# Phase one of a two-branch transformer layer: first-norm products put off behind the second norms of later tiles, five tiles transposed on TensorE instead of eight, six single tiles instead of four

## The chip, the cores and the metric

The kernel runs on one core of one Trainium2 chip. The metric is device time in microseconds (us). Every run of this case was in the fast state and on one core; the granted TensorE clock of a run lay between 0.997 and 1.000. A ratio is the mean time of one kernel's fast runs over the mean time of the other's fast runs of the same rounds, so it is not quite the ratio of the medians quoted beside it. In the profiles TensorE is PE, VectorE DVE and ScalarE ACT; POOL and SP are two more engines, and here they issue the DMAs of phase one, each from a queue of its own.

## The reference, cut to what matters

```python
def _layernorm(x, axis=-1, eps=1e-05):
    m = jnp.mean(x, axis=axis, keepdims=True)
    v = jnp.var(x, axis=axis, keepdims=True)
    return (x - m) / jnp.sqrt(v + eps)

def _B_ref(x, w1, w2, w3, w4):              # x: (1, 2048, 1024), bf16
    h = _gelu(_layernorm(x, axis=-1) @ w1)  # w1: (1024, 1024)
    ...                                     # shifts of rows, @ w2, second MLP with w3, w4
x = A_x
xn = _layernorm(x, axis=-1)                 # the first norm
return x + _A_ref(xn, ...) + _B_ref(xn, ...)
```

Branch B normalizes the already normalized `xn` again. The kernel computes both norms from one set of statistics of `x`: the "first norm" gives `xn` (needed in phase two and in branch A), the "second norm" gives the input of the product with `w1`.

## The kernel before: the parts that matter

The 2048 rows are 16 tiles of 128. Phase one computes `gelu(norm2(x) @ w1)`. For that each tile's second norm must be transposed: tiles 0 to 7 by matmuls with an identity on TensorE, tiles 8 to 15 by a DMA transpose that SP issues. The first norm of a tile, made on VectorE, does three things at once: it keeps `xn` on the chip, POOL writes it to a scratch in DRAM, and it frees the tile's x buffer, so that SP may load the x tile ten places on.

```python
def load_x(n):
    if n < NT:
        xts[n] = ring.tile([P, D], BF16, tag="xt", bufs=10, name=f"xt{n}")
        nc.sync.dma_start(xts[n][:], x_v[:, n, :])
# ... loads of x 0..9, w1, w2 are issued here ...

def norm_stats(n, part=None):                       # cut
    nc.vector.bn_stats(st[:, 0, :], xt[:, 0:512])
    nc.vector.bn_stats(st[:, 1, :], xt[:, 512:1024])
    nc.vector.bn_aggr(mv[:], st[:])
    nc.vector.scalar_tensor_tensor(ab[:], ...)
    nc.gpsimd.tensor_tensor(rr[:], ab[:], neghalf[:], op=ALU.pow)
    if n >= NPE:
        nc.gpsimd.tensor_scalar(nm2[:], ...)

def norm2(n, xn2T, jj):                             # second norm
    if n < NPE:                                     # on VectorE (NPE = 8)
        nc.vector.tensor_scalar(xn2[:, c], xts[n][:, c], ...)
    else:                                           # on ScalarE, then a DMA transpose
        nc.scalar.activation(xn2[:], xts[n][:], ACTF.Identity, bias=nm2[:], scale=rr[:, 1:2])
        nc.sync.dma_start_transpose(xn2T[:, jj], xn2[:])

def norm1(n):                                       # first norm
    nc.vector.tensor_scalar(xn, xts[n][:], ...)
    nc.gpsimd.dma_start(xn_v[:, n, :], xn)          # 256 KB to DRAM
    load_x(n + 10)                                  # 256 KB from DRAM, on SP's queue
    if n in (12, 15):
        load_w3()

for n in range(1, NPE):                             # tiles 1..7
    norm_stats(n + 1, 0); norm2_of(n); norm_stats(n + 1, 1)
    if n > 1:
        norm1(n - 2)                                # two tiles behind
    if n < 4:
        stage1(n - 1, 1, ...)                       # single tiles 0, 1, 2 (then 3)
for n0 in range(4, NT, 2):                          # pairs (4,5) .. (14,15)
    stage1(n0, 2, tiles2[n0], between)              # 8 groups of 8 matmuls, one GELU each
```

A "group" below is eight matmuls into one PSUM tile, ended by one GELU on ScalarE; a tile or a pair has eight groups.

## Time and profile before

| | before |
|---|---|
| time, median of 6 runs (lowest, highest) | 1521.69 us (1520.39, 1524.99) |
| span of the profiled run | 1519.6 us |
| TensorE busy | 1508.8 us, 99% |
| phase one's products on TensorE | 8.38 to 69.39 us |

From the page of the kernel before: busy times by engine (us, share of the span, instructions), the granted TensorE clock in 40 slices (9 is 90% or more), and the chain of work that ended last, by engine.

```profile
PE 1508.8 (99%) x9781; PEld 808.3 (53%) x9853; DVE 546.2 (36%) x1137; ACT 506.7 (33%) x1147; POOL 179.4 (12%) x248
...
PEclk9999999999999999999999999999999999999999
...
PE 98%; DMA 1%; issue 0%; DVE 0%; ACT 0%; SPq 0%; POOL 0%
```

TensorE is the bound: 99% busy, at full clock, and 98% of the chain. Only a wait of TensorE, or work taken from it, can move the time by much.

From the timeline of TensorE before (start in us, length, engine, line, operation, count). L292 is the transposing matmul, L303 the product with w1, L377 the first product of phase two.

```profile
16.03 0.39 PE L292 MATMUL ps<-c_ident_sb,xn 128*128 128x128 bf16 x4
16.25 0.61 PE L303 MATMUL ps<-xn2T,w_sb 128*128 128x128 bf16 x8
16.70 0.39 PE L292 MATMUL ps<-c_ident_sb,xn 128*128 128x128 bf16 x4
...
32.71 36.84 PE L303 MATMUL ps<-xn2T,w_sb 128*128 128x256 bf16 x336
69.39 5.78 PE L377 MATMUL ps<-w_sb,hTB 128*128 128x512 bf16 x25
```

Here is one tile's transposes, two halves of four matmuls, and then the pairs: 36.8 us of matmuls without a gap that the profile counts, and phase two at 69.39. Four transposing matmuls take 0.22 us (16.03 to 16.25), eight 128-column products 0.45 us (16.25 to 16.70).

Four stretches of the kernel before: start:end, length, then busy us and instruction count of PE, PEld, DVE, ACT and POOL, the granted clock, the mean busy share of the 16 DMA engines (it can come out a little over 1), and GB/s.

```profile
core 0: us, PE busy (x) PEld busy (x) DVE busy (x) ACT busy (x) POOL busy (x), PEclk, DMA share, GB/s
17.00:23.00 6.00, 5.99 (x106) 5.75 (x103) 5.85 (x14) 4.41 (x16) 3.78 (x5) 1.00 1.05 389
23.00:28.00 5.00, 4.92 (x74) 4.49 (x71) 4.84 (x12) 3.81 (x12) 2.71 (x5) 1.00 0.85 303
28.00:46.00 18.00, 18.00 (x175) 16.24 (x173) 17.43 (x43) 13.84 (x29) 14.40 (x24) 1.00 0.88 195
46.00:54.00 8.00, 8.00 (x75) 7.16 (x74) 1.44 (x4) 6.03 (x12) 3.23 (x6) 1.00 1.05 272
```

The last two columns are the ones to keep. DMA runs at 389 and 303 GB/s up to 28 us, when w2 and the x tiles come in, and less after that, when the transposes start.

### The profile page before, as it was taken

To read this page: it belongs to the slowest core of one execution; us is meant where nothing else is said; L and a number is where in the kernel's file an instruction comes from. 1 tells how busy PE (TensorE), PEld (TensorE's weight loads), DVE (VectorE), ACT (ScalarE), POOL (GpSimd) and SP (SyncE) were. 2 spreads that over 40 slices of the span, in tenths; PEclk is the share of its full clock that TensorE was granted. 3 is DMA by queue.
4 is the path that set the end of the run, shared out by engine and by line. 5 is a ranking of instruction groups with operands and counts; after the bars stand their busy time and mean duration, and the time that the engine had idled before them with its cause. 6 is when DMAs were issued, how large, how long until landed. Compare 5 with 4: busy or idle time off the path is not lost.

```text
span 1519.6 us, 24277 instructions
## 1 busy us (share of the span) xinstructions
PE 1508.8 (99%) x9781; PEld 808.3 (53%) x9853; DVE 546.2 (36%) x1137; ACT 506.7 (33%) x1147; POOL 179.4 (12%) x248
## 2 busy tenths in 40 slices
PE   9999999999999999999999999999999999999998
PEld 7844444445444444444466645654665555445555
DVE  7382230100120122222246614651664266416542
ACT  6533203013022011111256614650663266326630
POOL 5231020211111231100000010001000100010001
PEclk9999999999999999999999999999999999999999
DMA  8799762353355887532499947992997389628611
GB/s 283 157 266 317 220 174 93 136 201 111 126 169 141 198 281 255 192 133 70 137 240 253 238 117 189 244 238 79 228 240 190 118 223 217 185 76 209 175 46 53
DMA packets 306459, 274.20 MB, mean 180 GB/s; under 512 B 153787, under 2 KB 274128, under 8 KB 306088
## 3 DMA queue, kind: packets, MB, share of 16 engines
q1 hardware_dynamic: 284168, 189.92, 49.3%
q0 software_dynamic: 22032, 82.63, 15.9%
q8 instruction: 79, 1.29, 0.4%
q14 instruction: 36, 0.29, 0.1%
q10 hardware_dynamic: 144, 0.07, 0.0%
HBM read 190.98 MB, written 46.19 MB: 156 GB/s over the span
## 4 chain that ended last, share of the span: by engine, by line
PE 98%; DMA 1%; issue 0%; DVE 0%; ACT 0%; SPq 0%; POOL 0%
PE ps L651 30%; PE pso L709 14%; PE ps L577 14%; PE ps L519 13%; PE ps L545 13%; PE ps L377 4%; PE ps L303 3%; PE psS L666 2%; PE psO L690 2%; PE ps L836 1%; PE ps L469 1%; PE ps L434 0%; PE gps L448 0%; DMA wt<-in_A_Wq_dram 0%; DMA PT<-Pn 0%; PE warm L320 0%
## 5 line engine op out<-in xcount | busy, mean ns | idle before, releaser
L651 PE MATMUL ps<-hTb,wt 128*128 128x396 bf16 (+3 forms) x2528 | 500.4, 343 | 0.3 <-DMA wt<-in_A_Wq_dram 0.3
L651 PEld LDWEIGHTS <-wt 128*128 128x128 bf16 x2528 | 232.2, 98 | 167.6 <-DMA wt<-in_A_Wq_dram 0.7
L577 PE MATMUL ps<-wt,xT 128*128 128x512 bf16 x1003 | 220.1, 379 | 1.1
L709 PE MATMUL pso<-wo_sb,oX 128*128 128x512 bf16 x938 | 209.3, 379 | 1.2 <-issue 0.2
L519 PE MATMUL ps<-xn3T,w_sb 128*128 128x512 bf16 x896 | 196.2, 379 | 0.0
L545 PE MATMUL ps<-w_sb,h3T 128*128 128x512 bf16 x873 | 194.3, 379 | 1.2
L577 PEld LDWEIGHTS <-xT 128*128 128x128 bf16 x1024 | 100.2, 98 | 120.8
L520 ACT ACTIVATE h3T<-ps 128x512 bf16<-128x512 f32 x112 | 66.9, 597 | 290.4 <-PE ps L519 289.5
L709 PEld LDWEIGHTS <-oX 128*128 128x128 bf16 x960 | 92.6, 98 | 108.2
L657 ACT CAST KT<-ps 128x396 bf16<-128x396 f32 (+3 forms) x160 | 82.3, 514 | 186.9 <-PE ps L651 184.2
L545 PEld LDWEIGHTS <-h3T 128*128 128x128 bf16 x896 | 87.0, 98 | 103.4
L519 PEld LDWEIGHTS <-w_sb 128*128 128x128 bf16 x896 | 86.6, 98 | 102.1
L672 DVE TENSOR_REDUCE sums<-sm 99x4 f32<-99x396 f32 (+2 forms) x176 | 97.6, 555 | 113.0 <-ACT sm L670 113.0
L659 ACT ACTIVATE QT<-ps 128x396 bf16<-128x396 f32 (+3 forms) x160 | 84.2, 527 | 119.1 <-PE ps L651 102.0
L668 DVE TENSOR_TENSOR sm<-psS,c_mask_reg_sb 99x396 f32<-99x396 f32 x160 | 91.3, 571 | 86.3 <-PE psS L666 85.7
L579 ACT CAST Vs<-ps 128x512 bf16<-128x512 f32 x64 | 37.5, 587 | 233.1 <-PE ps L577 174.9
L670 ACT ACTIVATE sm<-sm 99x396 f32<-99x396 f32 (+2 forms) x176 | 92.9, 528 | 63.7 <-DVE sm L668 60.7
L583 DVE CAST Vs<-ps 128x512 bf16<-128x512 f32 x64 | 44.3, 692 | 170.0 <-PE ps L577 158.0
L678 DVE TENSOR_TENSOR Pn<-sm,rs 99x396 bf16<-99x396 f32 (+2 forms) x176 | 99.0, 562 | 7.2 <-DMA PT<-Pn 1.1
L546 DVE TENSOR_TENSOR R<-ps,R 128x512 f32<-128x512 f32 x32 | 21.9, 690 | 180.9 <-PE ps L545 166.6
L716 POOL DMA_DIRECT2D out_dram<-ot x30 | 16.4, 547 | 584.0 <-DVE ot L715 578.2
L715 DVE TENSOR_TENSOR ot<-pso,Rt 128x512 bf16<-128x512 f32 (+1 forms) x33 | 22.3, 676 | 172.3 <-PE pso L709 166.9
(120 smaller groups left out, 1072.0 us busy)
## 6 DMA issues: line engine op xcount, KB each, us to landing
wt<-in_A_Wq_dram SPq DMA_DIRECT2D x76, 512.0 KB
wt<-in_A_Wk_dram SPq DMA_DIRECT2D x76, 512.0 KB
wt<-in_A_Wv_dram POOLq DMA_DIRECT2D x24, 1024.0 KB, 6.5
V_scratch<-Vs SPq DMA_DIRECT2D x32, 512.0 KB
V<-V_scratch SPq DMA_DIRECT2D x32, 384.0 KB
R_scratch<-x POOLq DMA_DIRECT2D x16, 512.0 KB, 3.9
R<-R_scratch SPq DMA_DIRECT2D x16, 512.0 KB
R_scratch<-R POOLq DMA_DIRECT2D x16, 512.0 KB, 3.2
```

Source lines behind the costliest of these rows:

```text
L519: nc.tensor.matmul(ps[:].rearrange("p (n t) -> p n t", t=P), w3_sb[:, k, f * P:(f + 1) * P], xn3T[tb][:, :, k, :], start=(k == 0), stop=(k ...
L520: nc.scalar.activation(h3T[:, f, :], ps[:], ACTF.Gelu_apprx_tanh)
L545: nc.tensor.matmul(ps[:], h3T[:, f, j * P:(j + 1) * P], w4_sb[:, f, ch * 512:(ch + 1) * 512], start=(f == 0), stop=(f == FT - 1))
L577: nc.tensor.matmul(ps[:], xT[:, m4 * 4 + j, k, :], wv[:, k, :], start=(k == 0), stop=(k == KT - 1))
L651: nc.tensor.matmul(ps[:, :nb] if flat else ps[:, :nb].rearrange("p (t c) -> p t c", t=nt), w[:, k, hh * P:(hh + 1) * P], B["rhs"](k), star ...
L657: nc.scalar.copy(o, i)
L659: nc.scalar.mul(o, i, scale)
L668: nc.vector.tensor_tensor(sm[:T, :, :T], S3, t["mask"][:].unsqueeze(1).to_broadcast((T, 4, T)), op=ALU.add)
L670: nc.scalar.activation(e[:T, :, :T], sm[:T, :, :T], ACTF.Exp, scale=LN2)
L672: nc.vector.tensor_reduce(ss, e[:T, :, :T], axis=AX.X, op=ALU.add)
L678: nc.vector.tensor_tensor(Pn[:T, :, :T], e[:T, :, :T], rs[:T, :].unsqueeze(2).to_broadcast((T, 4, T)), op=ALU.mult)
L709: nc.tensor.matmul(self.ps[:, :self.w], self.oX[self.gl // 3][:, h, self.gl % 3 * P:(self.gl % 3 + 1) * P], wo_sb[:, h, self.cc], start=(h ...
```

## The change

The intent, as the code reads: TensorE's last waits in phase one are for second norms and their transposes, so VectorE should make second norms earlier and first norms later (they are needed only after 69 us). With second norms earlier, tiles 5, 6 and 7 can go through the DMA transposes, which takes 24 matmuls from TensorE. Tiles 4 and 5 become single tiles, so that tile 4 need not wait for tile 5. To make room, x has nine buffers instead of ten.

```diff
-                    NPE = 8
+                    NPE, NDVE = 5, 8          # transposed on TensorE; second norm on VectorE
...
-   xts[n] = ring.tile([P, D], BF16, tag="xt", bufs=10, name=f"xt{n}")
+   xts[n] = ring.tile([P, D], BF16, tag="xt", bufs=9, name=f"xt{n}")
...
-                        load_x(n + 10)
+                        load_x(n + 9)
...
-                    for n in range(1, NPE):
-                        if n > 1:
-                            norm_stats(n + 1, 0)
+                    def s_and_n(n):
+                        norm_stats(n + 1, 0)
                         norm2_of(n)
-                        norm_stats(n + 1, 1 if n > 1 else None)
-                        if n > 1:
-                            norm1(n - 2)
...
+                    norm2_of(1)
+                    norm_stats(2)
+                    stage1(0, 1, tiles2[0], trs(1, 5))
+                    s_and_n(2)
+                    stage1(1, 1, tiles2[0], trs(2, 4), 1)
+                    s_and_n(3)
+                    stage1(2, 1, tiles2[2], trs(3, 4))
+                    s_and_n(4)
+                    s_and_n(5)
+                    stage1(3, 1, tiles2[2], trs(4, 4), 1)
+                    s_and_n(6)
+                    norm1(0)
+                    norm2_of(7)
+                    norm_stats(8)
+                    stage1(4, 1, tiles2[4], {})
+                    norm1(1)
+                    norm1(2)
+                    norm_stats(9)
                     def prep(n):
                         norm2_of(n)
-                        norm_stats(n + 1)
-                        norm1(n - 2)
+                        if n + 2 < NT:
+                            norm_stats(n + 2)
+                        for m in range(2 * n - 13, 2 * n - 11) if n < 12 else range(n - 1, n + n // 15):
+                            norm1(m)
+                    stage1(5, 1, tiles2[4], {2: [lambda: prep(8)], 6: [lambda: prep(9)]}, 1)
+                    for n0 in range(6, NT, 2):
+                        stage1(n0, 2, tiles2[n0], {2: [... prep(n0 + 4)], 5: [... prep(n0 + 5)]} if n0 + 4 < NT else {})
```

The diff is cut: the statistics ring grows from 6 to 12 buffers, x tile 9 leaves the loads that are issued at the start, and the removed loops of pairs are left out.

More of the change, by code (lines that the diff above doesn't have):

```diff
@@ L243 @@
                         nc.sync.dma_start(w2_sb[:, 2 * i:2 * i + 2, :], w2_v[:, 2 * i:2 * i + 2, :])
-                    for n in range(7, 10):
+                    for n in range(7, 9):
                         load_x(n)
@@ L254, in norm_stats @@
                         if n not in stats:
-                            stats[n] = [ring.tile(shape, F32, tag=tag, bufs=6, name=f"{tag}{n}") for tag, shape in (("st", [P, 2, 6]), ("mv", [P, 2]), ("ab", [P, 2]), ("rr", [P, 2]), ("nm2", [P, 1]))]
+                            stats[n] = [ring.tile(shape, F32, tag=tag, bufs=12, name=f"{tag}{n}") for tag, shape in (("st", [P, 2, 6]), ("mv", [P, 2]), ("ab", [P, 2]), ("rr", [P, 2]), ("nm2", [P, 1]))]
                         st, mv, ab, rr, nm2 = stats[n]
@@ L264, in norm_stats @@
                         nc.gpsimd.tensor_tensor(rr[:], ab[:], neghalf[:], op=ALU.pow)
-                        if n >= NPE:
+                        if n >= NDVE:
                             nc.gpsimd.tensor_scalar(nm2[:], mv[:, 0:1], rr[:, 1:2], -1.0, op0=ALU.mult, op1=ALU.mult)
@@ L270, in norm2 @@
                         xn2 = ring.tile([P, D], BF16, tag="xn2")
-                        if n < NPE:
+                        if n < NDVE:
                             for c in (slice(0, 512), slice(512, 1024)) if n == 0 else (slice(0, 1024),):
@@ L275, in norm2 @@
                             nc.scalar.activation(xn2[:], xts[n][:], ACTF.Identity, bias=nm2[:], scale=rr[:, 1:2])
+                        if n >= NPE:
                             nc.sync.dma_start_transpose(xn2T[:, jj], xn2[:])
@@ L338 @@
                     load_consts(4)
-                    for n in range(1, NPE):
-                        if n > 1:
-                            norm_stats(n + 1, 0)
+                    def s_and_n(n):
+                        norm_stats(n + 1, 0)
                         norm2_of(n)
-                        norm_stats(n + 1, 1 if n > 1 else None)
-                        if n > 1:
-                            norm1(n - 2)
-                        if n < 4:
-                            stage1(n - 1, 1, tiles2[(n - 1) // 2 * 2], {5: [lambda n=n: tr(n, 0)], 6: [lambda n=n: tr(n, 1)]}, (n - 1) % 2)
@@ L348, with trs @@
-                    stage1(3, 1, tiles2[2], {4: [lambda: tr(4, 0)], 5: [lambda: tr(4, 1)], 6: [lambda: tr(5, 0)], 7: [lambda: tr(5, 1)]}, 1)
+                        norm_stats(n + 1, 1)
+                    def trs(n, c):
+                        return {c: [lambda: tr(n, 0)], c + 1: [lambda: tr(n, 1)]}
+                    norm2_of(1)
[3 more added lines that the diff above has]
+                    stage1(1, 1, tiles2[0], trs(2, 4), 1)
@@ L351, in prep @@
                         norm2_of(n)
-                        norm_stats(n + 1)
-                        norm1(n - 2)
-                    for n0 in range(4, NT, 2):
-                        between = {c: [] for c in range(KT)}
-                        if n0 + 4 < NT:
-                            between[1 + 2 * (n0 == 4)] += [lambda n0=n0: prep(n0 + 4)]
-                            between[4 + 2 * (n0 == 4)] += [lambda n0=n0: prep(n0 + 5)]
-                        if n0 == 4:
-                            for c in range(4):
-                                between[1 + 2 * c // 2 + (c > 1)] += [lambda c=c: tr(6 + c // 2, c % 2)]
-                        stage1(n0, 2, tiles2[n0], between)
@@ L364 @@
-                    for n in (NT - 2, NT - 1):
-                        norm1(n)
+                        if n + 2 < NT:
[4 more added lines that the diff above has]
+                    for n0 in range(6, NT, 2):
+                        stage1(n0, 2, tiles2[n0], {2: [lambda n0=n0: prep(n0 + 4)], 5: [lambda n0=n0: prep(n0 + 5)]} if n0 + 4 < NT else {})
```

## The prediction

> **What bounds the kernel.** TensorE: by the page's first part busy 1508.8 of 1519.6 us (99%), granted clock 1.00, 98% of the chain that ended last. Phase one is 8.4 to 69.4 us of TensorE's timeline. Inside it the chain leaves TensorE only at 7.7-11.8 us (first tiles) and 24.15-27.0 us, where it goes through ScalarE (PSUM copies of transposed tiles 4 and 5, GELUs). So the change can move the time by a few us at most.
>
> **TensorE's work** (durations from the timeline):
> - 24 of 64 transposing matmuls go; a half tile of four took 0.22 us: -1.34 us. Tiles 5, 6, 7 go to DMA transposes.
> - Pair (4,5) becomes singles. Eight 128-column matmuls took 0.447 us (56 ns each; the Trainium skill, "TensorE: Matmul & The Clock Gate", section "Wait — 56ns, not 53.3ns?", gives 55.6 ns; the trace agrees), eight 256-column ones 0.873. A pair costs 6.99 us, two singles 7.16: +0.17 us.
> - Net -1.17 us.
>
> **Waits removed.** After each tile transposed at groups 5 and 6, the next tile's first group took 0.60 instead of 0.45 us, because the copy of the second half (0.59 us on ScalarE) came late; pair (4,5) lost about 0.2 us. Transposes at groups 4 and 5 hide the copy. Tiles 2-4 gain about 0.12 us each: -0.5 us in all.
>
> **Waits added.**
> - Tile 2's transposes are wanted near 15.6 us, but its second norm ended at 15.9 and nothing ahead of it changes: +0.35 us.
> - In this trace a DMA transpose took 3.5 us from issue to landing for tile 8, and 4.6-6.6 us for tiles 9-11, mixed with loads of x and scratch writes. Putting off first norms (0.45 us each) buys VectorE little: the next second norm waits about 1.1 us for POOL's power anyway, so its cadence falls from 2.7 to only about 2.5 us. My estimates: tile 5 issued at 23.2, landed 27-28.5, wanted 29.4; tile 7 issued 28, landed 31.5-34, wanted 33.0; tile 9 landed 39-40.5, wanted 39.9. Tile 5 makes it, 7 and 9 are on the edge: +0.4 us.
>
> **Off the path.** The 16 first-norm products move later on VectorE, which idles from 47.4 to 71.4 us; they are needed after 70. Nine x buffers instead of ten: load 9 is issued behind the first put-off product (about 26 us), needed near 30. ScalarE's 8 second norms (1.24 us) start about 1 us earlier; four PSUM buffers hide them.
>
> **Sum.** -1.17 - 0.5 + 0.35 + 0.4: about -0.7 us with rounding and noise, 0.05%. The rest is unchanged and TensorE-bound. Three runs of before spread 1.2 us, more than the gain.
>
> Predicted time 1520.8 us, range 1519.3 to 1522.3. Faster by over 2%: 0.005; within 2%: 0.99; slower: 0.005.
>
> **What would show each step.** Transposing matmuls 40 instead of 64; matmuls up by 40. Phase one ends on TensorE's timeline near 68.6 instead of 69.4 us; pair (6,7) starts near 33.0. The chain no longer passes ScalarE's copies at 24-27 us; instead perhaps short TensorE waits at tile 2's transposes, and at the first matmul of pair (6,7) or (8,9), released by a DMA. First-norm products end on VectorE near 47 us.
>
> **What would make it wrong.** Transposes landing 2 us or more later than estimated (SP issues them in order behind x loads that wait for put-off first norms): then phase one is 1-2 us longer, the time about 1522.5. If they land early and the copies hide fully, the gain is up to 1.5 us. Over 5 us anywhere would mean I missed a stage.

## More of the kernel before

The timeline of SP before, from 31 to 48 us: the last load of x, then six DMA transposes, nothing between them.

```profile
31.03 0.33 SPq L233 DMA_DIRECT2D xt<-in_A_x_dram  x1
33.24 15.60 SPq L276 DMA_TRANSPOSE xn2T<-xn  x6
```

## The result, and the profile after

| | before | after |
|---|---|---|
| time, median of 6 runs (lowest, highest) | 1521.69 us (1520.39, 1524.99) | 1528.32 us (1526.85, 1529.55) |
| ratio | | 1.0041, 95% interval 1.0028 to 1.0054 |
| span of the profiled run | 1519.6 us | 1525.9 us |
| first product of phase two on TensorE | 69.39 us | 74.23 us |
| TensorE's waits for DMA transposes in phase one | none | 4.3 us |
| from there to the end | 1450.2 us | 1451.7 us |

The change makes the kernel slower by 0.4%, clear of the noise, where a gain of 0.05% was forecast. Of the 6.3 us between the two profiles 4.84 lie in phase one. The other 1.5 lie behind it, where the program is the same. That stretch took 1449.5 to 1451.7 us in all profiles but one, so this part is within what one run differs from another.

From the page after: busy times, and the chain by engine.

```profile
PE 1513.1 (99%) x9893; PEld 808.2 (53%) x9893; DVE 546.2 (36%) x1137; ACT 505.2 (33%) x1149; POOL 177.1 (12%) x248
...
PE 96%; DMA 2%; DVE 1%; POOL 0%; SPq 0%; issue 0%; ACT 0%; ACTq 0%; POOLq 0%
```

TensorE has 4.3 us more busy time although it has less work, and DMA and VectorE have entered the chain. (The busy time counts a matmul at half clock at its full length, and some matmul records are missing from a trace: 9781 instructions before, 9893 after, where the programs differ by 40.)

The timeline of TensorE after. Lines are shifted: L304 is the product with w1, L293 the transposing matmul, L388 phase two.

```profile
15.48 0.40 PE L293 MATMUL ps<-c_ident_sb,xn 128*128 128x128 bf16 x4 [0.20 <-DVE xn L273]
...
24.43 7.76 PE L304 MATMUL ps<-xn2T,w_sb 128*128 128x128 bf16 x136
32.51 7.73 PE L304 MATMUL ps<-xn2T,w_sb 128*128 128x128 bf16 x72 [0.33 <-ACT hTB L306]
43.60 8.70 PE L304 MATMUL ps<-xn2T,w_sb 128*128 128x256 bf16 x64 [3.36 <-DMA xn2T<-xn]
53.27 21.12 PE L304 MATMUL ps<-xn2T,w_sb 128*128 128x256 bf16 x192 [0.97 <-DMA xn2T<-xn]
74.23 16.13 PE L388 MATMUL ps<-w_sb,hTB 128*128 128x512 bf16 x74
```

Up to 40 us things go as planned: tile 2's transposes wait 0.20 us for the second norm, the single tiles 4 and 5 run through but for 0.33 us (at tile 5's last group, behind ScalarE), and the matmuls of tiles 0 to 7 are done at 40.2 us. Then pair (8,9) waits 3.36 us for its DMA transpose, and its 64 matmuls take 8.70 us instead of about 7.0; pair (10,11) waits another 0.97 us.

The granted clock (third column from the right) explains the 8.70 us: three stretches of the kernel after, columns as before.

```profile
42.00:44.00 2.00, 0.40 (x3) 0.28 (x3) 1.93 (x6) 0.05 (x1) 1.70 (x4) 0.84 1.05 385
44.00:46.00 2.00, 2.00 (x11) 1.44 (x10) 2.00 (x5) 0.39 (x1) 1.69 (x4) 0.50 1.20 323
46.00:48.00 2.00, 2.00 (x17) 1.62 (x16) 1.93 (x6) 0.41 (x2) 1.88 (x4) 0.80 1.04 281
```

The clock falls to half for about 3.4 us (0.32 + 1.00 + 0.40 us lost in the three stretches, twice that at half clock). The Trainium skill, "TensorE: Matmul & The Clock Gate", section "What's actually happening", says that an idle window of about 3.4 us brings the clock to half, and here the wait was 3.36 us long. The runs below agree only in part. A half clock of 3.4 us also follows a wait of 3.62 us (after_again), but in e2 it follows one of 2.21 us, and none follows waits of 2.90 us (e1) and 3.21 us (e2), so the length of the wait alone does not tell. Before, no such stretch is in the middle of the run.

The same four stretches of time after:

```profile
17.00:23.00 6.00, 6.00 (x111) 6.00 (x109) 5.25 (x13) 4.39 (x16) 1.68 (x3) 1.00 0.78 284
23.00:28.00 5.00, 5.00 (x93) 5.00 (x91) 4.08 (x11) 3.69 (x13) 2.26 (x3) 1.00 0.61 114
28.00:46.00 18.00, 14.32 (x159) 12.39 (x157) 15.46 (x36) 10.17 (x25) 11.77 (x22) 0.93 0.96 252
46.00:54.00 8.00, 7.03 (x61) 5.93 (x60) 4.51 (x12) 4.65 (x9) 6.09 (x11) 0.95 1.09 257
```

This shows what the change did to the DMA traffic. Between 17 and 28 us the DMA engines moved 284 and 114 GB/s instead of 389 and 303, and were idle up to 39% of the time; from 28 to 46 us they moved 252 instead of 195 GB/s and were busy 96% instead of 88%, and from 46 to 54 us 109% instead of 105%. Loads and writes moved later, into the time of the transposes (and three more transposes came to them).

SP's queue after, from 31 to 48 us:

```profile
36.72 1.44 SPq L233 DMA_DIRECT2D xt<-in_A_x_dram  x2
38.26 1.46 SPq L277 DMA_TRANSPOSE xn2T<-xn  x1
39.81 1.87 SPq L233 DMA_DIRECT2D xt<-in_A_x_dram  x2
41.78 6.20 SPq L277 DMA_TRANSPOSE xn2T<-xn  x2
```

Before, the transposes stood alone on SP's queue. Now a pair of x loads stands ahead of tile 9's transpose (38.26) and ahead of tile 10's (41.78), and tile 11's comes behind tile 10's. Tile 9's second norm was ready at 35.01 us, its transpose was issued 3.25 us later. Tile 11's was ready at 41.51, but SP was busy with issuing tile 10's until 44.36 (2.58 us, where tiles 5 to 9 took 1.2 to 1.8) and began with tile 11's at 44.45, 2.94 us late.

The chain of waits after, in order of time (start, length, what):

```profile
30.11 4.32 DMA xt<-in_A_x_dram
34.45 0.69 DVE st L258
...
38.26 5.30 DMA xn2T<-xn
43.60 0.85 PE ps L304 x4
44.45 8.68 DMA xn2T<-xn
53.27 21.12 PE ps L304 x192
```

Read it from the end: pair (10,11) at 53.27 waited for a transpose that had been issued at 44.45 and took 8.68 us to land; pair (8,9) at 43.60 for one issued at 38.26 that took 5.30. (The chain puts the issue at 44.45 down to TensorE; by SP's own records, above, it came right behind the issue of tile 10's transpose.) Between the two uppermost lines and 38.26 the chain is less sure: it names a second norm on ScalarE, but tile 9's had been ready since 35.0. In SP's queue above, the issue at 38.26 follows two x loads; the first of them was issued at 36.72, when the first norm of tile 3 had ended (36.69), and that stood on VectorE behind statistics (34.45) that had waited for a load of x issued at 30.11. So a late load made statistics late, these a first norm, this the next loads, and these the transpose. The load issued at 30.11 is that of x tile 10; before, it was issued at 17.47.

### The profile page after: what moved, and what is told of

The parts are those of the page before. It is cut to its first block, busy times and chain, and to the rows that moved or that the text cites. A ratio compares the mean times of both kernels' runs of the same rounds, so it can differ in the third digit from the quotient of the medians.

```text
span 1525.9 us, 24433 instructions
## 1 busy us (share of the span) xinstructions
PE 1513.1 (99%) x9893; PEld 808.2 (53%) x9893; DVE 546.2 (36%) x1137; ACT 505.2 (33%) x1149; POOL 177.1 (12%) x248
## 4 chain that ended last, share of the span: by engine, by line
PE 96%; DMA 2%; DVE 1%; POOL 0%; SPq 0%; issue 0%; ACT 0%; ACTq 0%; POOLq 0%
PE ps L662 30%; PE pso L720 15%; PE ps L588 14%; PE ps L530 13%; PE ps L556 13%; PE ps L388 4%; PE psS L677 2%; PE psO L701 2%; PE ps L304 1%; DMA xn2T<-xn 1%; DMA xt<-in_A_x_dram 1%; PE ps L847 1%; PE ps L480 1%; DMA PT<-Pn 1%; PE gps L459 0%; PE ps L445 0%
```

## The experiments

Two theories at the outset, with the runs that tell them apart. **A, queue order:** SP issues in order, and transposes stand behind x loads that wait for put-off first norms. **B, traffic:** a DMA transpose lands late when loads and writes run beside it, whoever issues them; putting off the first norms moved their loads and writes into the time of the transposes. Later theories are named where they are tested: D is the three more DMA transposes; C is the clock in e2, and in e5 something else, the writes alone.

All eleven runs gave correct results. The kernels of one row block ran on one chip and share their runs of the kernel before.

| run | time, median (lowest to highest) | before, same chip, 11 runs | ratio, 95% interval | phase two starts | waits of TensorE for DMA transposes in phase one |
|---|---|---|---|---|---|
| e1_pool_x | 1527.19 (1525.71 to 1528.76) | 1522.37 | 1.0030 (1.0013 to 1.0047) | 75.40 | 2.9 |
| e2_fill | 1529.03 (1523.87 to 1532.63) | 1522.37 | 1.0038 (1.0017 to 1.0059) | 79.15 | 5.4 |
| e3_npe8 | 1526.90 (1524.81 to 1531.31) | 1522.37 | 1.0035 (1.0015 to 1.0054) | 71.24 | 1.6 |
| e4_order | 1524.88 (1523.43 to 1525.88) | 1522.37 | 1.0014 (0.9998 to 1.0031) | 70.73 | see text |
| e5_keep16 | 1521.59 (1520.88 to 1525.72) | 1521.35 | 1.0009 (0.9996 to 1.0022) | 68.11 | 0 |
| e6_late_writes | 1521.36 (1520.51 to 1523.34) | 1521.35 | 1.0002 (0.9989 to 1.0015) | 68.91 | 0 |
| e7_both | 1521.18 (1520.24 to 1523.08) | 1521.35 | 0.9999 (0.9986 to 1.0012) | 67.95 | 0 |
| e8_before_late | 1521.33 (1520.47 to 1530.18) | 1521.35 | 1.0011 (0.9993 to 1.0029) | 70.09 | 0 |
| after_again | 1528.04 (1525.00 to 1531.08) | 1521.51 | 1.0034 (1.0020 to 1.0049) | 76.04 | 5.6 |
| e7_again | 1520.58 (1520.10 to 1522.50) | 1521.51 | 0.9992 (0.9979 to 1.0005) | 67.89 | 0 |
| e9_dup | 1524.42 (1524.12 to 1528.84) | 1521.51 | 1.0013 (1.0000 to 1.0026) | 72.08 | 2.1 |

The second table is taken from the records of DMA issue and landing in the traces: us from the start of a transpose's issue by SP to its last landing, by tile. The issue itself is in it: 1.2 us at the least, 5.3 at the most (e2, tile 11). A dash is a tile transposed on TensorE.

| tile | before | after | e1 | e3 | e6 | e7_again | e8 | e9 |
|---|---|---|---|---|---|---|---|---|
| 5 | - | 3.2 | 3.2 | - | 3.2 | 5.5 | - | - |
| 6 | - | 3.4 | 3.4 | - | 4.8 | 6.2 | - | - |
| 7 | - | 4.4 | 4.7 | - | 3.6 | 4.1 | - | - |
| 8 | 3.6 | 5.2 | 7.7 | 4.0 | 3.2 | 3.4 | 3.8 | 3.6 |
| 9 | 4.6 | 5.3 | 4.6 | 6.8 | 4.2 | 4.7 | 3.1 | 4.4 |
| 10 | 6.7 | 6.8 | 6.7 | 5.9 | 4.1 | 3.2 | 3.1 | 5.7 |
| 11 | 6.2 | 8.7 | 6.7 | 7.7 | 3.8 | 3.0 | 4.1 | 7.1 |
| 12 | 5.4 | 5.2 | 5.1 | 5.3 | 3.0 | 3.1 | 3.1 | 6.3 |
| 13 | 5.3 | 7.7 | 5.6 | 6.1 | 3.1 | 3.1 | 3.0 | 7.4 |

### e1_pool_x: x loads off SP's queue

```diff
-  nc.sync.dma_start(xts[n][:], x_v[:, n, :])
+  (nc.sync if n < 9 else nc.gpsimd).dma_start(xts[n][:], x_v[:, n, :])
```

> The kernel after, with the loads of x tiles 9 to 15 issued by POOL instead of SP; SP's queue then holds only the transposes. Theory A (SP issues in order, and the transposes of tiles 9 to 11 stand behind x loads that wait for put-off first norms): the transpose of tile 9 is issued within 1 us of its second norm (about 35 us instead of 38.3), TensorE's 3.4 us wait at pair (8,9) falls under 0.5 us, phase one ends at 69 to 70 instead of 74.2 us, time 1522 to 1524. Rival B (a DMA transpose is slow whenever other DMA traffic runs beside it, whoever issues that): the transpose is issued early but lands no earlier than about 42 us, phase one ends after 72 us, time 1526 or more.

Measured: 1527.19 us, and phase two starts at 75.40 us. Tile 9's transpose was issued 0.02 us after its second norm, so the queue order was repaired. Waits of TensorE in phase one:

```profile
PE ps L304 <- ACT hTB L306: 3.9, 5, 1.6
PE ps L304 <- DMA xn2T<-xn: 2.9, 1, 2.9
```

What follows: repairing the queue order did not bring the time back, as theory A in its strict form expects. The waits only moved: the loads, now issued later by POOL (x tiles 9 to 12 by 1.5 to 3.0 us) and slower to land (x tile 11 took 7.1 us from issue to landing, 4.3 in after), starve the statistics, ScalarE stands before a second norm and TensorE behind its GELUs (3.9 us), and tile 14's transpose took 11.8 us. B's number for tile 9 (landing not before 42 us) was wrong too, it landed at 40.9; the time was as B expected. Since the run also delays the loads, it is no clean test of A; e6, where the loads stay ahead of the transposes, is the better one. This agrees with the Trainium skill, "DMA: Bandwidth & Descriptors", section "Issuing engines are not separate DMA queues": DMAs of all issuing engines run on the same 16 DMA engines and interleave.

### e2_fill: keeping the clock up in the wait

```diff
   for n0 in range(6, NT, 2):
+      if n0 == 8:
+          pf = psum0.tile([P, 4, P], F32, tag="tr")
+          for i in range(14):
+              nc.tensor.matmul(pf[:]..., wz[:, :P], wz[:], start=(i == 0), stop=(i == 13))
       stage1(...)
```

> The kernel after, with 14 matmuls on zeros (about 3.0 us) put ahead of pair (8,9), where TensorE stood idle for 3.4 us and then ran at half clock for 3.4 us. Theory C (the half clock costs 1.7 us of the loss): no stretch at clock 0.5 in phase one, phase one ends 1.5 to 2 us earlier, time 1526.5. Theory A (the second wait, for tile 11's transpose landing at 53.1 us, sets the end of phase one, so the slow clock only fills that wait): the clock stays at 1.00, the wait at pair (10,11) grows from 1.0 to about 2.7 us, phase one ends within 0.4 us of 74.2, time unchanged at 1528.

Measured: 1529.03 us with a spread of 8.8 us, and in the profile:

```profile
40.72 3.19 PE L379 MATMUL pf<-wz 128*128 128x512 bf16 x14
46.11 8.83 PE L304 MATMUL ps<-xn2T,w_sb 128*128 128x256 bf16 x64 [2.21 <-DMA xn2T<-xn]
58.15 21.16 PE L304 MATMUL ps<-xn2T,w_sb 128*128 128x256 bf16 x192 [3.21 <-DMA xn2T<-xn]
```

The filler ran (40.72), but the transposes landed later still in this run (tile 9 at 46.1, tile 11 at 58.0 us), TensorE waited 2.2 and 3.2 us, and the trace's clock record has a half-clock stretch at 46.2 to 49.6 us all the same. Inconclusive: what the half clock costs by itself stays open. In the profile of after, the chain shows that the landing of tile 11 set the start of pair (10,11), so there the slow matmuls of pair (8,9) were hidden in that wait.

### e3_npe8: eight tiles on TensorE, first norms still put off

```diff
-  NPE, NDVE = 5, 8
+  NPE, NDVE = 8, 8
-  stage1(4, 1, tiles2[4], {})
+  stage1(4, 1, tiles2[4], trs(5, 4))
-  stage1(5, 1, tiles2[4], {2: [prep(8)], 6: [prep(9)]}, 1)
+  stage1(5, 1, tiles2[4], {1: [tr(6, 0)], 2: [tr(6, 1), prep(8)], 4: [tr(7, 0)], 5: [tr(7, 1)], 6: [prep(9)]}, 1)
```

> The kernel after with tiles 5 to 7 transposed on TensorE again (eight, as before); first norms put off and nine x buffers as in after. If the put-off first norms with their late x loads alone make the loss (theory A in its strict form): transposes of tiles 9 to 11 still land late, TensorE still waits 2 us or more before pair (8,9) or (10,11), time 1526 or more. If the three more DMA transposes are needed for it (theory D: together with the loads they fill the queue): no wait over 0.5 us, phase one ends at 69.5 to 70.5, time 1521.5 to 1523.

Measured: 1526.90 us, a loss as large as that of the whole change (1.0035). The profiled run was the fastest of its six (1524.81), with one DMA wait of 1.6 us; the slower ones have no profile. Stretches of this kernel, columns as before:

```profile
23.00:28.00 5.00, 5.00 (x93) 5.00 (x91) 4.08 (x11) 3.69 (x13) 2.19 (x3) 1.00 0.03 8
28.00:46.00 18.00, 16.39 (x202) 14.84 (x200) 15.99 (x38) 13.46 (x33) 12.44 (x23) 1.00 0.97 261
```

What follows: the three more DMA transposes (theory D) are not needed for the loss. Without them the DMA engines stand still from 23 to 28 us (8 GB/s, where before moved 303), and are full from 28 us on. What is left of the change, the put-off first norms with nine x buffers and two more single tiles, is enough for a loss; the next run puts the first norms back.

### e4_order: the new TensorE plan, the old order of first norms

```diff
-  xts[n] = ring.tile(... bufs=9 ...)          # and load_x(n + 9), first loads up to 8
+  xts[n] = ring.tile(... bufs=10 ...)         # load_x(n + 10), up to 9; statistics ring 6
   s_and_n(2)
+  norm1(0)
   stage1(1, ...)
   s_and_n(3)
+  norm1(1)
   ...                                         # norm1(n - 2) after s_and_n(n), up to n = 7
   def prep(n):
       norm2_of(n)
-      if n + 2 < NT: norm_stats(n + 2)
-      for m in range(...): norm1(m)
+      norm_stats(n + 1)
+      norm1(n - 2)
```

> The kernel after with the first norm two tiles behind the second norm and ten x buffers, as before; five tiles on TensorE and six single tiles are kept. Theory A: the x loads are all issued by about 31 us as before, no transpose waits behind one, phase one ends at 68 to 69.5 us with at most 0.5 us of waits for DMA, time 1520.5 to 1522. Theory D (three more DMA transposes are what the queue can't take): waits of 1 us or more at pair (6,7) or (8,9), phase one ends after 71 us, time 1524 or more.

Measured: 1524.88 us, ratio 1.0014. The median lies in D's range, the end of phase one (70.73) between the two expectations.

```profile
34.22 0.61 PE L304 MATMUL ps<-xn2T,w_sb 128*128 128x128 bf16 x8 [1.82 <-ACT hTB L306]
35.78 35.11 PE L304 MATMUL ps<-xn2T,w_sb 128*128 128x256 bf16 x320 [0.96 <-ACT xn L275]
```

No later pair waits, so most of the loss is gone. But tile 5's last group waits 1.8 us behind ScalarE, which waited for the statistics of tile 8 and could not serve the GELUs, and pair (6,7) 0.96 us more; the profile puts this second wait down to ScalarE, but by the landing records tile 7's transpose landed at 35.74, just before the start at 35.78. Tile 7 is one of the three more DMA transposes, so D has a share here. What follows: the put-off was there for a reason, for with the old order VectorE is late for the new plan; and undoing it, with ten x buffers again, removes the waits behind 40 us.

### e5_keep16: all x loads early

```diff
-  xts[n] = ring.tile([P, D], BF16, tag="xt", bufs=9, name=f"xt{n}")
+  xts[n] = xn_keep[n // 4][:, n % 4]          # x is loaded into the tile that keeps xn
-  for n in range(7, 9): load_x(n)
+  for n in range(7, 16): load_x(n)
-  load_x(n + 9)                               # in norm1, which now works in place
```

> The kernel after, with x loaded into the tile that will keep the first norm (made in place), so that all sixteen loads are issued at once and land by about 28 us; the scratch writes are as in after. Theory B (a DMA transpose lands late when loads and writes run beside it): with the loads out of the stretch from 28 to 47 us, and only the 16 writes left, a transpose takes 3 to 5.5 us to land instead of 5 to 9, TensorE waits under 1.5 us for DMA in all, phase one ends at 69 to 71 us, time 1521.5 to 1524. Theory A (queue order alone, already hurt by the previous runs) expects the same early end, so this run tells B only from a third, C: that put-off writes alone are what delays the transposes; then waits of over 3 us stay and the time is 1526 or more.

Measured: 1521.59 us, ratio 1.0009; phase two starts at 68.11 us, TensorE waits for no DMA, and transposes of tiles 8 to 13 land in 3.6 to 4.4 us. B's range for the time holds, and phase one ended earlier than B said. C (the writes alone) falls. Queue order goes with the loads, so the run does not tell A from B. One of the five runs took 1525.72 us; it has no profile.

### e6_late_writes: the scratch writes behind the transposes

```diff
   def norm1(n):
       nc.vector.tensor_scalar(xn, xts[n][:], ...)
-      nc.gpsimd.dma_start(xn_v[:, n, :], xn)
+      xn_writes.append((xn_v[:, n, :], xn))
   ...                                         # behind the last pair of phase one:
+  gate = big.tile([P, 1], BF16)
+  nc.gpsimd.tensor_copy(gate[:], hTB[:, 0, 2 + 12 * P:3 + 12 * P])   # waits for a GELU of pair (12,13)
+  for dst, xn in xn_writes:
+      nc.gpsimd.dma_start(dst, xn)
```

> The kernel after, with the sixteen scratch writes of the first norm issued together behind a small POOL instruction that waits for a GELU of pair (12,13), at about 59 us; loads of x as in after. Theory B: transposes land in 3 to 5.5 us, tile 9 is still issued about 3 us late behind its loads (38 us) and lands near 42, TensorE waits 1 to 2.5 us for DMA instead of 4.3, phase one ends at 70 to 72 us, time 1522.5 to 1525. Theory A (queue order alone): tile 11 lands after 50 us as before and the end stays at 74 us.

Measured: 1521.36 us, ratio 1.0002, better than B's range; phase two starts at 68.91.

```profile
32.80 7.59 PE L305 MATMUL ps<-xn2T,w_sb 128*128 128x128 bf16 x72 [0.28 <-ACT hTB L307]
40.95 28.12 PE L305 MATMUL ps<-xn2T,w_sb 128*128 128x256 bf16 x256 [0.56 <-ACT hTB L307]
```

TensorE's two short waits are for ScalarE. SP's queue still has the x loads ahead of tile 9's transpose, which was issued 1.5 us after its second norm and landed in 4.2 us; tiles 12 and 13 have no load beside them and landed in 3.0 and 3.1. Only the writes were taken away, on another queue than the transposes, and the loss is gone: this is theory B, and strict A falls here. The traffic worked in two ways. Tile 9 landed at 40.90 us instead of 43.55; 1.51 us of this is an earlier issue, as the x loads ahead of it came earlier (x tile 10 landed in 3.1 us instead of 4.3), and 1.15 us a shorter landing.

### e7_both, and once more e7_again beside after_again

e5 and e6 together.

> Both of the two before: loads early, writes late, so that hardly any copy runs beside the transposes of tiles 6 to 13. Theory B: each of these lands 3 to 4 us after its issue, no wait of TensorE for DMA over 0.3 us, phase one ends at 68.0 to 69.3 us, earlier than the 69.4 of before, time 1520.5 to 1522, at or just under before. If waits of over 1 us remain, the DMA traffic is not the cause, and the transposes are slow for a reason of their own (three more of them).

> The kernel after once more, unchanged, beside the next two on one chip. All theories: 1526.5 to 1529.5 us. Its transposes of tiles 8 to 13 land 5 to 9 us after issue again; where exactly TensorE waits may shift by a tile or two, the end of phase one lies between 73 and 76 us.

> Loads early and writes late once more, on the same chip as the kernel after. Theory B: 5 to 8 us faster than after, at or up to 1.5 us under before (phase one ended 1.4 us earlier than in before); no TensorE wait for a DMA in phase one.

Measured: 1521.18 and 1520.58 us; the kernel after beside it, on the same chip, 1528.04. No matmul of phase one waits after 28 us (profile of e7_again):

```profile
27.82 40.24 PE L304 MATMUL ps<-xn2T,w_sb 128*128 128x128 bf16 x404
67.89 12.47 PE L394 MATMUL ps<-w_sb,hTB 128*128 128x512 bf16 x55
```

Tiles 10 to 13 land in 3.0 to 3.2 us. Tiles 5 and 6, which now stand behind the loads of x 9 to 15, take 5.5 and 6.2 and still come in time; tile 9's 4.7 us, with no load or write beside it, has no explanation here. after_again waited 3.6 us at pair (8,9) and 2.0 us at pair (12,13), not (10,11): which transpose comes too late changes from run to run, that some do does not.

In both profiles phase one ends 1.4 to 1.5 us earlier than before, which is what the change was for. Its first product also started earlier, at 7.89 and 8.16 us instead of 8.38, so from there on the gain is 0.95 and 1.28 us. Over the whole kernel that is 0.1%, and the intervals (0.9986 to 1.0012, 0.9979 to 1.0005) include 1: e7 clearly beats after, and is not shown to beat before.

### e8_before_late: a control

The edit of e6 on the kernel before.

> A control: the kernel before with the scratch writes put off in the same way. Theory B: its transposes, which took 3.1 to 7.0 us, take 3 to 4.5 us; but TensorE did not wait for them, so the end of phase one stays at 69.0 to 69.5 us and the time is that of before within 1 us.

Measured: 1521.33 us, ratio 1.0011, one of six runs at 1530.18 (no profile). Transposes of tiles 9 to 13 landed in 3.0 to 4.1 us instead of 4.6 to 6.7, and nothing was gained, as expected: before, TensorE did not wait for them. Phase two starts at 70.09, where 69.0 to 69.5 was expected; the profile has a wait of 0.5 us for w1, and its first product started 0.1 us later.

### e9_dup: the converse

```diff
   nc.gpsimd.dma_start(xn_v[:, n, :], xn)
+  if 6 <= n < 14:
+      nc.sync.dma_start(dup_v[:, n, :], xn)   # 256 KB to a scratch of its own, kernel before
```

> The converse: the kernel before, TensorE's and VectorE's work and order unchanged, with eight more writes of 256 KB (the first norm of tiles 6 to 13 a second time, to a scratch of its own, from SP's queue) between its transposes from about 34 to 56 us. Theory B (copies beside transposes): transposes of tiles 9 to 13 land 5.5 to 9 us after issue, TensorE waits for DMA by 1.5 us or more in all, phase one ends at 71 to 74 us, time 1523.5 to 1527. If the rearranged first norms or the buffers were the cause and not the traffic: the end stays at 69.4 us and the time within 1 us of before.

Measured: 1524.42 us, ratio 1.0013 (1.0000 to 1.0026); phase two starts at 72.08.

```profile
56.97 7.15 PE L307 MATMUL ps<-xn2T,w_sb 128*128 128x256 bf16 x64 [1.17 <-DMA xn2T<-xn]
65.10 7.15 PE L307 MATMUL ps<-xn2T,w_sb 128*128 128x256 bf16 x64 [0.98 <-DMA xn2T<-xn]
```

Nothing but traffic was added to the kernel before, and TensorE now waits 2.1 us for DMA transposes, which took 5.7 to 7.4 us for tiles 10 to 13 (tile 9's 4.4 us was under the range expected). Some of this is queue order, since tile 13's transpose was issued 1.7 us late behind a write. The profiled run was the slowest of five, and 3.1 us of its loss are waits for weights in a later phase, which were not followed up; so of the time only part belongs to the transposes.

## Why the prediction was wrong

Point by point:

- **TensorE bound, and 1.17 us of its work removed: right.** With the waits gone (e7_again) phase two starts 1.50 us earlier, 1.28 counted from the first product. The prediction's sum without its DMA term is -1.17 - 0.5 + 0.35 = -1.32 us.
- **Copies hidden by transposing at groups 4 and 5: right.** The chain after has no ScalarE copy at 24 to 27 us, and the seven groups behind tile 2's transposes took 3.12 us on TensorE (16.39 to 19.51) instead of 3.29 (16.92 to 20.21). Tile 2's wait was 0.20 us instead of 0.35.
- **The cadence of second norms, 2.5 us: right.** Tile 5's transpose was issued at 22.82 (said: 23.2), tile 7's at 27.96 (said: 28) and landed at 32.4 (said: 31.5 to 34).
- **"Tile 9 landed 39-40.5 ... 7 and 9 are on the edge: +0.4 us": this step failed.** Tile 9 landed at 43.55, tile 11 at 53.13; TensorE waited 4.3 us for DMA in the profile, 5.6 in another, and phase two started 4.84 us later instead of 0.8 earlier. For tile 9 the issue was what the estimate had wrong: its 5.30 us from issue to landing lie within the 3.5 to 6.6 us carried over from before, but the issue came 3.25 us behind the second norm, after two x loads. For tile 11 both were wrong: issued 2.94 us late, it took 8.68 us to land. The times of before belonged to the queue and the traffic of before.
- **"Off the path. The 16 first-norm products move later on VectorE": this is where it came from.** As VectorE work they were off the path (they ended at 50.65 us, where 47 was said, and were needed after 74). But each carries a 256 KB write and releases a 256 KB load. Put off, these left the DMA engines idle to 39% between 23 and 28 us, and came back from 28 to 54 us beside the transposes, when the engines were busy 96% and more. Runs e5 and e6 each take one half of this traffic away and the loss is gone (e5 the queue order with it, e6 not). e9 adds traffic to before, and waits for transposes of 2.1 us appear; its loss in time is barely clear of noise (interval from 1.0000). In e1 the loads went to another queue, and the waits only moved.
- The clause "what would make it wrong" named late transposes behind waiting x loads, and sized them at 1 to 2 us. Order on SP's queue was there (tile 9 lost 3.25 us to it, tile 11 2.94), but repairing it in e1 gained nothing clear, and with the order left as it was e6 lost nothing.

What stays open: the share of the nine x buffers, since no run has put-off first norms and ten buffers (with ten, x tile 10 would wait for the first norm of tile 0, which ended at 26.80 us, and not for that of tile 1, at 30.08); the cost of the half clock by itself (e2), why a run now and then takes 7 to 9 us more than the others (one of 11 of before in the first set, one of six of e8), and how the 6.6 us between the medians divide over runs that have no profile.

## What to carry to other kernels

An instruction that is off the critical path by its engine may still not be moved freely: list the DMAs that it issues or releases, and ask when these will run and beside what. A DMA transpose has no fixed time to land; here it was 3.0 us undisturbed and up to 12.4 us among copies, so budget it from a trace with the traffic it will have, and put loads that can go early and writes that can go late outside its stretch. When a queue's order looks guilty, leave it and take traffic from another queue away, as e6 did: if the wait goes, the order alone was not the cause.

## What the Trainium skill lacked or had wrong

- "Advanced Engine Details and Errata", section "X-Bar Transpose (TRN2)": it says that transpose DMAs on this chip are as fast as regular ones and expects 350 to 400 GB/s. Not so here for 128x1024 bf16 tiles between places in SBUF. Two stretches of the kernel after, the first with plain loads, the second with one transpose alone (share of DMA and GB/s at the end):

```profile
18.00:20.00 2.00, 2.00 (x40) 2.00 (x37) 1.73 (x5) 1.32 (x6) 0.69 (x1) 1.00 1.05 389
24.00:25.80 1.80, 1.80 (x36) 1.80 (x34) 1.60 (x3) 1.67 (x6) 0.66 (x1) 1.00 0.76 146
```

  The loads made 389 GB/s at a share of 1.05; the transpose, 256 KB, 146 GB/s at 0.76, so about half as many bytes for the same DMA time (192 against 370 GB/s at a full share). This is one tile alone; no run has a long row of transposes with nothing else.
- "DMA: Bandwidth & Descriptors", section "Rules for kernel authors": it says that a transpose next to ordinary DMAs needs nothing. That may hold for the result (all runs were correct); its cost in time: 3.0 to 3.2 us from issue to landing without copies beside it, 4.6 to 8.7 us for tiles 9 to 13 of the kernels before and after, among 256 KB loads and writes, and 12.4 us at worst (e2, tile 11, of which 5.3 were its issue).
- "VectorE: DVE Perf Modes", section "The three transpose paths": it gives 1309 ns for a 128x128 block by DMA and 390 ns on TensorE. For eight blocks in one go: 3.0 us by DMA, undisturbed, and 0.45 us of TensorE's time for two halves of four matmuls (0.22 us each), pipelined, beside two copies of 0.59 us each on ScalarE; one block's latency is not what such a choice should be costed by.
